# Softmax features stored head by head, with kv and numerator blocks of 4 or 5 heads instead of 8, and two kv accumulation banks instead of three

## Chip, cores, metric

One core of one Trainium2 chip. The metric is the device time of one execution in microseconds (us), from several executions of each kernel. TensorE is called PE, VectorE DVE, ScalarE ACT, GpSimd POOL. Changed and unchanged kernel are always timed in alternating rounds on the same chip.

## What is computed

Two layers, each a linear-attention block A and a gated bilinear MLP B, on x of 2048 x 576 (32 heads of 18, MLP width 4608). Cut to what matters:

```python
def _A_ref(x, wqkv, w_phi, wo):                      # H = 32, Dh = 18
    q, k, v = ...                                    # x @ wqkv, per head
    pq = einsum("bhsd,hdf->bhsf", q, w_phi);  pk = same of k
    phi_q = concat([softmax(pq), softmax(-pq)], -1)  # two branches of 18: 36 features a head
    phi_k = concat([softmax(pk), softmax(-pk)], -1)
    kv = einsum("bhsf,bhsd->bhfd", phi_k, v);  z = sum over s of phi_k
    num = einsum("bhqf,bhfd->bhqd", phi_q, kv)
    den = einsum("bhqf,bhf->bhq", phi_q, z) + 1e-6
    return (num / den) @ wo                          # heads put together
x = x + A(ln(x));  x = x + B(ln(x));  x = x + A(ln(x));  x = x + B(ln(x))
```

A 128-token tile of phi has 32 x 36 = 1152 features, which TensorE takes as 9 blocks of 128. v carries a column of ones per head, so 19 columns a head give kv and z, and numerator and denominator, together.

## The kernel before

The program is written as threads that yield operations with an assumed duration. A list scheduler fixes the order of each engine's instructions when the kernel is built, so other durations or buffers mean another order. Eight PSUM banks are a pool (`pb`). The features are ordered branch 0 of all heads, then branch 1:

```python
self.dd = A("dd", [128, self.NSM, 2, D], BF16)            # phi: branch, then head, then 18
# kv of one 128-token tile: 9 blocks in 3 banks, each block against 8 heads (152 columns)
def kv_ops(self, sm, vxs, bi, bank, first, last):
    for i in range(3):
        k = 3 * bi + i
        g0 = 7 * k                                        # a block touches heads g0 .. g0+7 (mod 32)
        parts = ...                                       # split where the heads wrap: 10 matmuls a tile
        for j, h, n in parts:
            ops.append(... e.matmul(s.ps[:, bank, c0:c0 + CW * n], phi[:, 128 * k:128 * k + 128],
                                    s.vx[:, vxs, h:h + n, :], ...))
# after all tiles: keep of each block only the head that each feature row belongs to
    em = lambda e: e.tensor_tensor(BD[:, k0:k0 + 3], kv, mask9, ALU.mult)      # 3 times, DVE
# numerators of one tile: 12 matmuls of 152, 114, 76 or 38 columns
    e.matmul(s.ps[:, bank, c0:c0 + CW * n], s.eT[:, et, k, :], s.BD[:, k, j:j + n, :], ...)
# layer 1 accumulates kv over its 16 tiles in three PSUM banks held all the while
    gots = yield ("acqn", ["pb"], 3); s.kvb = [g_[1] for g_ in gots]
```

Layer 2 adds kv pair by pair of tiles into SBUF, inside layer 1's MLP. The MLP runs in 8 blocks of 256 tokens per layer: gate and up projections as pairs of half-height matmuls, then the down projection, whose weights stream in slices (`wdr`, `wdx`). Other work is slipped between.

## Time and profile before

| | before |
|---|---|
| median of 3 runs | 1109.35 us (1108.31 to 1110.13) |
| profiled span | 1108.5 us |
| PE / DVE / ACT / POOL busy | 97 / 52 / 33 / 27% of the span |
| MLP of layer 1 begins | 119.2 us |
| one full MLP block, layer 1 / layer 2 | 62.6 / 57.1 us |

The lines this rests on, and how to read them, stand in the prediction below. The blocks are bounded by the starts of MLP matmuls in the chain that ended last (layer 1: 239.5 to 302.1; layer 2: 709.5 to 766.6).

### The profile page before, as it was taken

What the parts mean: (1) busy time and instruction counts of PE and PEld (TensorE: products, weight loads), DVE (VectorE), ACT (ScalarE), POOL (GpSimd) and SP (SyncE); (2) the same over time, 40 slices, a digit from 0 to 9 for tenths busy, and PEclk for the clock granted to TensorE, in tenths of its full rate; (3) what the DMA queues carried; (4) which work ended last, traced back from release to release, by engine and by line L of the source; (5) the groups of instructions that cost most, each with busy time, mean ns of one, the idle gap of its engine ahead of it and who ended that gap; (6) DMA issues with size and microseconds to landing.
All of it is one profiled execution on the core that took longest, in us unless ns stands there. A gap on an engine that the chain in (4) does not pass through costs nothing.

```text
span 1108.5 us, 33749 instructions
## 1 busy us (share of the span) xinstructions
PE 1074.4 (97%) x15294; PEld 827.0 (75%) x15356; DVE 579.8 (52%) x1180; ACT 369.4 (33%) x870; POOL 297.5 (27%) x318
## 2 busy tenths in 40 slices
PE   6997999999999999999999989999999999999998
PEld 4676877868687787868587678686868686868685
DVE  6989645646374664636353676444445353524231
ACT  6776522414042332404232562131313030402120
POOL 4665404314161433302320252211212030300000
PEclk9999999999999999999999999999999999999999
DMA  8475326273733627170623313817271726352504
GB/s 171 120 236 237 57 63 175 29 205 47 187 66 115 125 46 189 32 211 21 161 67 97 97 24 47 216 35 216 36 216 35 194 58 189 62 177 53 177 29 140
DMA packets 185001, 129.06 MB, mean 116 GB/s; under 512 B 103322, under 2 KB 183706, under 8 KB 183706
## 3 DMA queue, kind: packets, MB, share of 16 engines
q1 hardware_dynamic: 184858, 126.91, 45.5%
q8 instruction: 120, 1.97, 0.7%
q14 instruction: 23, 0.19, 0.1%
HBM read 100.75 MB, written 2.36 MB: 93 GB/s over the span
## 4 chain that ended last, share of the span: by engine, by line
PE 85%; DVE 8%; DMA 2%; ACT 2%; POOL 1%; issue 1%; SPq 0%; POOLq 0%; DVEq 0%
PE ps L1481 49%; PE ps L1554 20%; PE ps L1011 6%; PE ps L1556 4%; PE ps L999 3%; PE ps L1342 2%; DVE st L943 1%; DMA wdr<-in_B_w_down_dram 1%; DVE ss L1166 1%; PE ps L1219 1%; DVE mxx L1086 1%; POOL dd L1177 1%; DVE mxmn L1044 1%; DVE hT L1529 1%; DVE mxmn L1039 1%
## 5 line engine op out<-in xcount | busy, mean ns | idle before, releaser
L1481 PE MATMUL ps<-xT,Wg 64*128 64x256 bf16 x4608 | 581.3, 269 | 0.8 <-ACT xT L981 0.8
L1481 PE MATMUL ps<-xT,Wu 64*128 64x256 bf16 x4608 | 580.0, 269 | 1.1 <-DVE hT L1529 0.8
L1481 PEld LDWEIGHTS ps<-xT,Wu 64*128 64x128 bf16 x4608 | 430.8, 94 | 31.0 <-DVE hT L1529 4.2
L1481 PEld LDWEIGHTS ps<-xT,Wg 64*128 64x128 bf16 x4608 | 428.0, 94 | 32.6 <-issue 3.3
L1527 ACT CAST hT<-ps 128x512 bf16<-128x512 f32 x288 | 168.3, 584 | 564.9 <-PE ps L1481 560.5
L1529 DVE TENSOR_TENSOR hT<-ps,hT 128x512 bf16<-128x512 f32 x288 | 196.8, 689 | 213.1 <-ACT hT L1527 210.8
L1554 PE MATMUL ps<-wdr,hT 128*128 128x512 bf16 x912 | 237.0, 380 | 2.0 <-DMA wdr<-in_B_w_down_dram 2.0
L1556 PE MATMUL ps<-wdr,hT 128*128 128x64 bf16 x960 | 185.0, 193 | 3.4 <-ACT hT L1527 0.7
L1554 PEld LDWEIGHTS ps<-wdr,hT 128*128 128x128 bf16 x960 | 93.9, 98 | 112.9 <-DMA wdr<-in_B_w_down_dram 4.2
L1481 PE MATMUL ps<-xT,Wr 64*128 64x256 bf16 x1152 | 174.5, 269 | 0.0
L1177 POOL TENSOR_TENSOR dd<-dd,ss 128x576 bf16<-128x576 bf16 x119 | 136.5, 1169 | 123.5 <-ACT ss L1173 118.6
L1147 POOL TENSOR_TENSOR dd<-xT,mxq 128x576 bf16<-128x576 bf16 x56 | 63.5, 1164 | 317.8 <-DVE mxq L1143 317.8
L1597 DVE TENSOR_TENSOR x_sb<-ps,x_sb 128x64 bf16<-128x64 f32 x32 | 7.0, 219 | 229.7 <-PE ps L1556 229.7
L971 POOL TENSOR_SCALAR xln<-x_sb,nmean,rstd 128x576 bf16<-128x576 bf16 (+1 forms) x99 | 60.7, 618 | 204.5 <-DVE nmean L956 107.2
L1166 DVE TENSOR_REDUCE ss<-dd 128x64 f32<-128x1152 bf16 x61 | 82.2, 1348 | 26.6 <-ACT dd L1160 23.7
L1556 PEld LDWEIGHTS ps<-wdr,hT 128*128 128x128 bf16 x960 | 94.0, 98 | 0.9 <-DVE hT L1529 0.7
L1481 PEld LDWEIGHTS ps<-xT,Wr 64*128 64x128 bf16 x1152 | 71.9, 94 | 6.6
L1554 PE MATMUL ps<-wdx,hT 128*128 128x512 bf16 x178 | 51.6, 380 | 0.9 <-DMA wdx<-in_B_w_down_dram 0.9
L943 DVE BATCH_NORM_STATS2 st<-x_sb 128x6 f32<-128x288 bf16 x120 | 46.0, 445 | 2.8 <-DMA x_sb<-in_A_x_dram 2.7
L1158 ACT ACTIVATE dd<-dd 128x576 bf16<-128x576 bf16 x49 | 33.5, 684 | 37.9 <-DVE dd L1058 27.5
L999 PE MATMUL ps<-Wq,xT 128*128 128x288 bf16 x300 | 40.1, 286 | 1.4 <-DVE dd L1058 1.4
L1011 PE MATMUL ps<-Wo,oT 64*128 64x288 bf16 x504 | 40.0, 283 | 0.0
(135 smaller groups left out, 960.4 us busy)
## 6 DMA issues: line engine op xcount, KB each, us to landing
wdr<-in_B_w_down_dram SPq DMA_DIRECT2D x240, 288.0 KB, 3.6
wdx<-in_B_w_down_dram SPq DMA_DIRECT2D x48, 288.0 KB, 3.7
Wg<-in_B_w_gate_dram SPq DMA_DIRECT2D x4, 1152.0 KB, 13.1
Wu<-in_B_w_up_dram SPq DMA_DIRECT2D x4, 1152.0 KB, 15.7
x_sb<-in_A_x_dram SPq DMA_DIRECT2D x8, 288.0 KB, 3.2
out_dram<-x_sb SPq DMA_DIRECT2D x16, 144.0 KB, 2.4
Wraw<-in_A_wqkv_dram SPq DMA_DIRECT2D x8, 144.0 KB, 3.0
xT<-xln SPq DMA_TRANSPOSE x58, 2.7
```

The source lines that it names most:

```text
L943: ops.append(Op(d_dve(288), (lambda e, j=j, h=h, src=src: e.bn_stats(st[:, sl[j], 6 * h:6 * h + 6], src)), reads=rd, writes=[("st", sl[j], ...
L971: em = [(lambda e, j=j, a=a, b=b, c=c: e.tensor_scalar(xln[:, sl[j], a:b], x_sb[:, ss[j], c:c + b - a], s.nmean[:, sl[j]:sl[j] + 1], rstd[ ...
L999: full = [Op(d_pe(N), (lambda e, k=k, h=h: e.matmul(s.ps[:, banks[h], 0:N], L[:, k, :], Wm[:, k, N * h:N * h + N], start=(k == 0 and fresh ...
L1011: out.append(Op(61, (lambda e, h=h, k=k, st=(i == 0 and k == 0), sp=(i == 1 and k == 3): e.matmul(s.ps[:, banks[h], 0:N], L[r, k, :], Wm[r ...
L1147: yield ("ops", "pool", [Op(1150, (lambda e, d=d, mb=mb: e.tensor_tensor(d, p3, mb, ALU.subtract)), reads=[("xT", st_), ("mq", mq, br)], w ...
L1166: Op(1265, (lambda e: e.tensor_reduce(ss[:, sm, :].rearrange("p (b g) -> p b g", b=2), e4, AX.X, ALU.add)), reads=s.ddk(sm, 0) + s.ddk(sm, ...
L1177: yield ("alt", [(eng, [Op(dur, (lambda e, ev=ev, rb=rb: e.tensor_tensor(ev, ev, rb, ALU.mult)), reads=s.ddk(sm, br) + [("ss", sm)], write ...
L1481: out.append(Op(54.3, (lambda e, bank=bank, cs=cs, lhsT=lhsT, rhs=rhs, st=st, sp=sp: e.matmul(ps[:, bank, cs].rearrange("p (a n) -> p a n" ...
L1527: yield ("ops", "act", [Op(480, (lambda e, gb=gb, p=p: e.copy(hT[:, p, :], ps[:, gb, :])), reads=[("gu", gb)], writes=[("hT", p)] + (s.raw ...
L1529: yield ("ops", "dve", [Op(600, (lambda e, ub=ub, p=p: e.tensor_tensor(hT[:, p, :], ps[:, ub, :], hT[:, p, :], ALU.mult)), reads=[("gu", u ...
L1554: ops = [Op(d_pe(512), (lambda e: e.matmul(s.ps[:, bank, 0:512], lhsT, s.wslot(slot)[:, fi, 0:512], start=(f == 0), stop=(f == NF - 1))), ...
L1556: Op(d_pe(64) + 3, (lambda e: e.matmul(s.ps[:, z, 64 * sl:64 * sl + 64], lhsT, s.wslot(slot)[:, fi, 512:576], start=(f == 0 and (sl == 0 o ...
```

## The change

The intent is fewer columns for PE. With both branches of a head side by side, a block of 128 features covers 4 or 5 heads instead of 8, so more than 40% of the columns, all of which the mask had set to zero, need not be computed. The core of the diff:

```diff
-        self.BD = A("BD", [128, NK, GH, CW], BF16)
-        self.kvacc = A("kvacc", [128, NK, KW], F32)
+        self.BD = A("BD", [128, 2, KC], BF16)              # KC = 5*4*19 = 4*5*19 = 380
+        self.kvacc = A("kvacc", [128, 2, KC], F32)
-        self.dd = A("dd", [128, self.NSM, 2, D], BF16)
+        self.dd = A("dd", [128, self.NSM, H, 2, DH], BF16)
+def kblock(k):
+    i = k // 2
+    return (7 * i, 4, 4 * CW * i) if k % 2 == 0 else (7 * i + 3, 5, 5 * CW * i)
 ...
-        de1 = dd[:, sm, 0, :]                              # likewise in every use of dd
+        de1 = dd[:, sm, :, 0, :]
 ...
-        for i in range(3):
-            k = 3 * bi + i
-            ...
+        for k in range(bi, NK, 2):
+            h, n, c0 = kblock(k)
+            ops.append(... e.matmul(s.ps[:, bank, c0:c0 + CW * n], phi[:, 128 * k:128 * k + 128],
+                                    s.vx[:, vxs, h:h + n, :], ...))
 ...
-        gots = yield ("acqn", ["pb"], 3)
+        gots = yield ("acqn", ["pb"], 2)
```

The masks follow (one memset and four mask operations more on POOL at the start, 1.6 us together), and kv, masking and accumulation run over 2 banks instead of 3.

## The prediction

> **What bounds the kernel now.** I read the page first: engine shares, the 40 slices and the shares of the chain that ended last.
>
> ```profile
> span 1108.5 us, 33749 instructions
> PE 1074.4 (97%) x15294; PEld 827.0 (75%) x15356; DVE 579.8 (52%) x1180; ACT 369.4 (33%) x870; POOL 297.5 (27%) x318
> ...
> PE   6997999999999999999999989999999999999998
> ...
> DVE  6989645646374664636353676444445353524231
> ...
> PEclk9999999999999999999999999999999999999999
> ...
> PE 85%; DVE 8%; DMA 2%; ACT 2%; POOL 1%; issue 1%; SPq 0%; POOLq 0%; DVEq 0%
> ```
>
> TensorE (PE) is the bound of nearly everything, at full granted clock. The exception is the first four slices (27.7 us each), where VectorE is as full as PE. A busy PE proves little, because matmul records overlap, so I took busy times over chosen stretches (the columns are stretch and length, then PE, weight load, DVE, ACT and POOL busy with instruction counts, clock, DMA share, GB/s):
>
> ```profile
> 75.00:90.00 15.00, 10.76 (x107) 8.04 (x106) 13.63 (x22) 8.85 (x25) 7.61 (x7) 1.00 1.02 427
> ...
> 176.00:612.00 436.00, 431.70 (x6510) 337.12 (x6536) 235.85 (x476) 138.43 (x316) 131.86 (x140) 1.00 0.45 108
> ...
> 709.00:1108.00 399.00, 392.54 (x5859) 300.62 (x5883) 161.19 (x314) 92.33 (x178) 60.00 (x64) 1.00 0.45 116
> ```
>
> There are two regimes. Until about 98 us the k softmax of layer 1 runs: DVE has 13.6 of 15 us, and PE waits. From 119 us on, PE streams the gated MLP with attention work slipped in between; in 176 to 612 only 4.3 of 436 us have no matmul in flight, while DVE, ACT and POOL have at least 46% of that stretch to spare. A nanosecond of matmul taken out of this regime should come off the end; one taken out before 98 us mostly should not.
>
> The third view is the groups by shape, for the two lines the change shrinks: L1219 (kv = phi_k^T times v) and L1342 (numerator = phi_q times the masked kv).
>
> ```profile
> L1342 PE MATMUL ps<-BD,eT 128*128 128x152 bf16 x192 | 25.3, 229 | 1.0 <-ACT eT L1318 1.0
> L1219 PE MATMUL ps<-vx,dd 128*128 128x152 bf16 x200 | 20.3, 230 | 3.1 <-POOL dd L1177 2.4 <-DVE dd L1177 0.8
> L1342 PE MATMUL ps<-BD,eT 128*128 128x114 bf16 x64 | 13.5, 211 | 0.0
> L1342 PE MATMUL ps<-BD,eT 128*128 128x38 bf16 x64 | 11.7, 183 | 0.0
> L1342 PE MATMUL ps<-BD,eT 128*128 128x76 bf16 x64 | 7.4, 198 | 0.0
> ```
>
> The means (183 to 230 ns) are latencies and must not be multiplied by counts. What a matmul takes from PE is the step from one start to the next, read from the timeline (start, length, group):
>
> ```profile
> 634.14 1.17 PE L1219 MATMUL ps<-vx,dd 128*128 128x152 bf16 x17 [0.40 <-POOL dd L1177]
> 635.15 2.61 PE L999 MATMUL ps<-Wq,xT 128*128 128x288 bf16 x20
> 637.60 0.78 PE L1342 MATMUL ps<-BD,eT 128*128 128x152 bf16 x12
> 638.22 1.39 PE L999 MATMUL ps<-Wq,xT 128*128 128x288 bf16 x10
> ```
>
> Seventeen kv matmuls (13 of 152 columns, 4 of 76) give way after 1.01 us, and the twelve numerator matmuls of one tile after 0.62 us.
>
> **What the Trainium skill says.** "TensorE: Matmul & The Clock Gate", section "Wait — 56ns, not 53.3ns?": back-to-back warm matmuls step by N/2.4 GHz plus about 2.5 ns, with a floor of about 25 ns. The trace agrees: 13 x 65.8 + 4 x 34.2 = 992 ns against 1.01 us, and 6 x 65.8 + 2 x 50 + 2 x 34.2 + 2 x 28 = 619 ns against 0.62 us; I use 28 ns as the floor, because the down projection's pair of 512 and 64 columns repeats about every 0.24 us (220.38, 220.62 in the timeline), which leaves about 28 ns for the 64. The same page, "Back-to-back issue gap", warns that pairs of weight load and matmul sustain only about 81 ns at 128 columns. If that held, short matmuls would gain nothing. The trace disagrees: nine 128-column transposes, each with its own weight load, start at 98.49 and give way at 99.00, 57 ns each. So weight loads should not hide the gain. "GPSIMD Engine Reference", "Performance pitfalls for Q7 kernels", puts a cost on reads whose inner step exceeds 8 bytes. The new layout strides the outer dimension only; the inner step stays one bf16, so POOL should not change.
>
> **The change part by part.**
> A 128-feature block used to touch 8 heads (branch 0 of all heads, then branch 1); with a head's two branches adjacent it touches 128/36 = 3.6 heads, in practice 4 or 5.
>
> kv, per tile of 128 tokens. Before: 9 blocks x 152 = 1368 columns in 10 matmuls, 8 x 65.8 + 2 x 34.2 = 595 ns. After: 5 x 76 + 4 x 95 = 760 columns in 9 matmuls, 5 x 34.2 + 4 x 42.1 = 339 ns. Saved: 256 ns.
>
> Numerator, per tile. Before: 619 ns, above. After: one block of 4 straddles head 16 and splits into 2 x 38, so 10 matmuls: 4 x 34.2 + 4 x 42.1 + 2 x 28 = 361 ns. Saved: 258 ns.
>
> Where they lie. There are 16 tiles in each of two layers. Layer 2's kv, and the numerators of both layers, run after 98 us, beside the PE-bound MLP or in the short chains around 101 to 119 and 634 to 651 us, where they stand on the chain too: 16 x (256 + 258 + 258) = 12.4 us. Layer 1's kv (16 x 256 = 4.1 us) runs before 98 us under DVE; the chain passes through it only now and then (0.6 to 0.8 us pieces), so I count a quarter, 1.0 us.
>
> Masking kv into BD at the end of layer 1 is 3 DVE operations of 626 ns on 456 elements, on the chain at 96 to 98 us. After: 2 on 380 elements, about 546 ns each (626 less 76 elements at 1.04 ns, an estimate from the DVE rows of 288 and 512 elements, 455 and 689 ns: 234 ns for 224 elements). Saved: 0.8 us. Layer 2's accumulation on DVE falls from 24 x 605 ns to 16 of about 526, 6.1 us of DVE, hidden behind PE: 0.
>
> Moves without expected cost: DVE, ACT and POOL now touch phi in runs of 18 with a stride of 36. The trace has such forms already: ACT writes v into runs of 18 at stride 19 in 401 ns, the same as a contiguous copy of 288 (401); DVE reads the numerator that way in 455 ns against 452. Four more mask-building POOL operations fall in the start-up: at most 1 us of POOL, probably hidden.
>
> Sum: 12.4 + 1.0 + 0.8 = 14.2 us off 1109.35, 1.3%.
>
> **Rivals.**
> (a) The gain gets lost in waits. If PE finishes earlier but each block's layer norm, weight slices or PSUM evacuation do not, PE idles instead. Against: PE waits in the steady part are tenths of a microsecond per block, and DMA moves about 110 GB/s with slices at 230 elsewhere. For: w_down waits stand on the chain (about 5 us of transfer at 357, 604 and 868), and the chain passes through the layer norm's statistics in each layer 2 block. A quarter lost gives 1098.5; all lost gives 1109.
> (b) The reordering matters more. Instruction order is fixed at build time from assumed durations, and tuning values chosen for the old order stay. New durations and a freed PSUM bank (two held through layer 1 instead of three) reshuffle the start-up, where between 17 and 105 us some 9 us pass with no matmul in flight (88 less the 79.0 us of PE busy in six stretches). With more banks k and q projections can run ahead: I allow 5 us better, and as much worse for a bad interleaving. "Perfetto Trace Analysis", "Optimization Strategy", says consistent bubbles can mean too little PSUM; here the bubbles sit behind DVE, so I expect little from the bank itself.
> (c) Strided phi makes POOL's multiplies (1169 ns, 119 of them) or ACT's exponentials slower. At 10% it adds about 0.25 us of POOL per tile; only layer 1's 16 tiles would show it, up to 4 us: 1099.
>
> **Range and chances.** From 14.2 I take off 2 us for (a) and the other frictions and leave (b) centred on zero: 12.2 us, 1097. The best case with all of layer 1's kv and a better start-up is 1087 to 1088; a bad reshuffle with losses is about 1107. A gain over 2% needs the time below 1087.2, beyond all the matmul time removed (16.5 us) plus 6 more: 6%. Slower by 2% needs 34 us of new waits: 1%.
>
> **What would show it.** The kv and numerator groups should appear with 76, 95 and 38 columns; a tile's numerators should give way after about 0.36 us, and its kv after 0.34. A layer 1 block (62.6 us from 239.5 to 302.1) should shrink by about 1.0 us, a layer 2 block (57.1 us from 709.5 to 766.6) by 0.5. The MLP should begin (119.25 us now) 1 to 3 us earlier, and the rows of POOL, ACT and DVE on phi keep their means. I am wrong if short matmuls step by well over 45 ns (weight loads bind), if blocks keep their length with new PE waits, or if the MLP begins at a time off by more than 5 us.

## The result

| | before | changed |
|---|---|---|
| median | 1109.28 us (4 runs) | 1095.01 us (4 runs, 1094.49 to 1096.43) |
| profiled span | 1108.5 us | 1092.9 us |
| MLP of layer 1 begins | 119.2 us | 115.5 us |
| first MLP block | 57.5 us | 58.8 us |
| full MLP block, layer 1 / layer 2 | 62.6 / 57.1 us | 61.6 / 56.6 us |

The ratio is 0.9877, 95% interval 0.9863 to 0.9891: 1.2% faster. A ratio here is the mean time of one kernel's fast runs over the mean of the other's in the same rounds, so not quite the ratio of the medians. Two repetitions of the changed kernel gave 0.9870 and 0.9875; the mean of the three is 0.9874, or 14.0 us of 1108.5. All runs of this study were in the fast state.

The page of the changed kernel (span, busy shares, chain by engine):

```profile
span 1092.9 us, 33612 instructions
PE 1061.4 (97%) x15260; PEld 811.7 (74%) x15260; DVE 571.2 (52%) x1171; ACT 367.7 (34%) x864; POOL 304.0 (28%) x327
...
PE 84%; DVE 9%; DMA 3%; ACT 2%; issue 1%; SPq 0%; POOL 0%
```

PE is the bound as before. The groups by shape for the numerators (L1351 is the old L1342):

```profile
L1351 PE MATMUL ps<-BD,eT 128*128 128x76 bf16 x128 | 17.1, 199 | 0.9 <-ACT eT L1327 0.9
L1351 PE MATMUL ps<-BD,eT 128*128 128x95 bf16 x128 | 14.8, 206 | 0.3 <-DVE BD L1296 0.3
...
L1351 PE MATMUL ps<-BD,eT 128*128 128x38 bf16 x64 | 6.6, 181 | 0.0
```

The three shapes are the predicted ones. The latencies fell by only 10%; the steps between starts tell the gain. Timeline of PE for one tile's numerators in the MLP, then, from the chain in order of time (start, length), one tile's kv:

```profile
219.27 0.52 PE L1351 MATMUL ps<-BD,eT 128*128 128x76 bf16 x10
219.63 0.38 PE L1563 MATMUL ps<-wdr,hT 128*128 128x512 bf16 x1
```

```profile
73.11 0.34 PE ps L1229 x9
```

The numerators give way after 0.36 us (predicted 0.361), and the kv after 0.34 us (predicted 0.339). Weight loads do not bind here: nine matmuls of 76 or 95 columns, each with its own load of 128 columns, step every 38 ns on average.

Busy times over MLP blocks, before: first block, a full block of layer 1, one of layer 2.

```profile
119.10:176.70 57.60, 57.39 (x864) 44.07 (x868) 27.32 (x57) 15.10 (x32) 12.95 (x14) 1.00 0.45 106
239.50:302.10 62.60, 62.34 (x942) 48.90 (x946) 35.48 (x74) 20.05 (x46) 20.80 (x22) 1.00 0.46 112
709.50:766.60 57.10, 56.72 (x849) 43.51 (x853) 25.62 (x52) 14.17 (x28) 11.52 (x12) 1.00 0.49 122
```

The same of the changed kernel:

```profile
115.40:174.40 59.00, 58.76 (x860) 44.33 (x862) 28.34 (x60) 14.26 (x30) 13.96 (x14) 0.97 0.41 104
359.50:421.10 61.60, 61.55 (x941) 47.88 (x940) 34.78 (x73) 20.06 (x46) 20.96 (x22) 1.00 0.46 114
753.50:810.10 56.60, 56.43 (x849) 43.00 (x848) 25.62 (x52) 14.17 (x28) 11.60 (x12) 1.00 0.48 122
```

A layer 1 block is 1.0 us shorter (two tiles of kv and two of numerators, 2 x 514 ns), a layer 2 block 0.5 us (two of numerators, 2 x 258 ns). The first four full blocks of layer 1 took 62.6 to 63.1 us before and 61.6 to 62.0 after. The first block did not shrink: it is 1.3 us longer, and its mean granted clock (third number from the right) is 0.97. That was not foreseen. The timeline of PE just before that block shows why. Before the change, two tiles' q projections (20 matmuls) stood between the two sets of six transposes:

```profile
113.78 0.56 PE L979 MATMUL ps<-ident,xln 128*128 128x128 bf16 x6
114.28 2.62 PE L999 MATMUL ps<-Wq,xT 128*128 128x288 bf16 x20
116.74 0.56 PE L979 MATMUL ps<-ident,xln 128*128 128x128 bf16 x6
```

After the change nothing does, because the projections were ordered earlier, and PE waits 2.01 us for a layer norm:

```profile
111.51 0.56 PE L993 MATMUL ps<-ident,xln 128*128 128x128 bf16 x6
114.09 0.57 PE L993 MATMUL ps<-ident,xln 128*128 128x128 bf16 x6 [2.01 <-DVE xln L985]
114.73 0.54 PE L1351 MATMUL ps<-BD,eT 128*128 128x76 bf16 x10
115.48 0.28 PE L1490 MATMUL ps<-xT,Wg 64*128 64x256 bf16 x1 [0.21 <-ACT xT L995]
```

Stretches of the same execution, where the clock is again the third number from the right:

```profile
111.60:115.45 3.85, 1.59 (x23) 0.97 (x21) 1.59 (x7) 2.94 (x9) 0.00 (x0) 1.00 0.30 44
115.45:117.00 1.55, 1.52 (x18) 1.15 (x20) 1.41 (x5) 0.13 (x1) 1.34 (x2) 0.60 0.00 0
117.00:119.00 2.00, 2.00 (x22) 1.47 (x20) 2.00 (x3) 0.00 (x0) 1.23 (x2) 0.50 0.00 0
```

PE had a matmul in flight for 1.59 of 3.85 us, most of that transposes, and for 3.4 us after that the clock was granted at one half, at the very moment the MLP began. The Trainium skill describes this ("TensorE: Matmul & The Clock Gate", "What's actually happening": idle drops the clock to half, judged over free-running windows of about 3.4 us); the trace agrees with the length of 3.4 us.

### The profile page after: what moved, and what is told of

The parts are those of the page before. It is cut to its first block, busy times and chain, and to the rows that moved or that the text cites. A ratio compares the mean times of both kernels' runs of the same rounds, so it can differ in the third digit from the quotient of the medians.

```text
span 1092.9 us, 33612 instructions
## 1 busy us (share of the span) xinstructions
PE 1061.4 (97%) x15260; PEld 811.7 (74%) x15260; DVE 571.2 (52%) x1171; ACT 367.7 (34%) x864; POOL 304.0 (28%) x327
## 4 chain that ended last, share of the span: by engine, by line
PE 84%; DVE 9%; DMA 3%; ACT 2%; issue 1%; SPq 0%; POOL 0%
PE ps L1490 49%; PE ps L1563 21%; PE ps L1025 6%; PE ps L1013 3%; PE ps L1565 3%; DVE ss L1180 2%; DVE st L957 2%; DMA wdr<-in_B_w_down_dram 1%; DVE mxx L1100 1%; PE ps L1351 1%; DMA wdx<-in_B_w_down_dram 1%; DVE hT L1538 1%; DMA x_sb<-in_A_x_dram 1%; PE ps L1229 1%; DVE mxmn L1058 1%; DVE mxmn L1053 1%
## 5 line engine op out<-in xcount | busy, mean ns | idle before, releaser
L1563 PE MATMUL ps<-wdr,hT 128*128 128x512 bf16 x960 | 244.7, 380 | 0.9 <-DMA wdr<-in_B_w_down_dram 0.9
L1191 POOL TENSOR_TENSOR dd<-dd,ss 128x576 bf16<-128x576 bf16 x119 | 139.1, 1190 | 124.0 <-ACT ss L1187 121.1
L1161 POOL TENSOR_TENSOR dd<-xT,mxq 128x576 bf16<-128x576 bf16 x56 | 63.6, 1166 | 306.8 <-DVE mxq L1157 306.8
L985 POOL TENSOR_SCALAR xln<-x_sb,nmean,rstd 128x576 bf16<-128x576 bf16 (+1 forms) x103 | 63.0, 616 | 196.4 <-ACT rstd L974 97.7
L1563 PE MATMUL ps<-wdx,hT 128*128 128x512 bf16 x192 | 54.3, 380 | 0.5 <-DMA wdx<-in_B_w_down_dram 0.5
L1187 ACT ACTIVATE ss<-ss 128x64 f32<-128x64 f32 x116 | 29.8, 257 | 31.5 <-DVE ss L1180 30.4
```

What stands on the lines that cost most here:

```text
L985: em = [(lambda e, j=j, a=a, b=b, c=c: e.tensor_scalar(xln[:, sl[j], a:b], x_sb[:, ss[j], c:c + b - a], s.nmean[:, sl[j]:sl[j] + 1], rstd[ ...
L1161: yield ("ops", "pool", [Op(1150, (lambda e, d=d, mb=mb: e.tensor_tensor(d, p3, mb, ALU.subtract)), reads=[("xT", st_), ("mq", mq, br)], w ...
L1191: yield ("alt", [(eng, [Op(dur, (lambda e, ev=ev, rb=rb: e.tensor_tensor(ev, ev, rb, ALU.mult)), reads=s.ddk(sm, br) + [("ss", sm)], write ...
L1563: ops = [Op(d_pe(512), (lambda e: e.matmul(s.ps[:, bank, 0:512], lhsT, s.wslot(slot)[:, fi, 0:512], start=(f == 0), stop=(f == NF - 1))), ...
```

## The experiments

Theory: PE's column time made the gain, in full after the start-up and in part within it. Rivals: the freed bank and the new order made it; part of the columns hides behind waits; the half clock gave some of it back. In the "columns back" runs the added matmuls are unknown to the scheduler (assumed duration 0). I compared the instruction lists: every engine has exactly the changed kernel's order, with only the added matmuls between (320 more among 15374 PE instructions with all columns back, nothing else different). They write unused PSUM columns, so results stay right. Differences in us below are differences of ratios times 1108.5. Each ratio has an interval of about 0.0015 (1.6 us) on either side unless given, so a difference of two is less certain still. The three sets of rounds ran on different chips; the first had no changed kernel in it, so its runs are set against the mean of the three.

### All columns given back

```diff
+        if extra:                                   # kv: columns 380.. of the bank, never read
+            for k, h0, n in ((bi, 0, 6), (bi + 2, 6, 6), (bi + 4, 12, 4)):
+                ops.append(Op(0, ... e.matmul(s.ps[:, bank, KC:KC + CW * n], phi[:, 128*k:128*k+128],
+                                              s.vx[:, vxs, h0:h0 + n, :], start=False, ...)))
+        for i, k in enumerate((0, 1, 6, 7)):        # numerators: columns 304.. of the two banks
+            ops.append(Op(0, ... e.matmul(s.ps[:, banks[i // 2], 16*CW:24*CW], s.eT[:, et, k, :],
+                                          s.BD[:, k % 2, 0:8*CW], start=False, ...)))
```

> The changed kernel, every instruction in the same order on every engine, with matmuls into unused PSUM columns that give back the columns the change took away: per tile 6 more for kv (4 of 114 columns, 2 of 76; about 268 ns) and 4 more of 152 for the numerators (about 263 ns). Theory (the gain is PE column time after the start-up): layer 2's kv gives 16 x 0.268 = 4.3 us, the numerators 32 x 0.263 = 8.4 us, layer 1's kv about a quarter of 4.3: 13.8 us in all, so about 1109 us, ratio to the kernel before 0.998 to 1.002. Rival (freed PSUM bank and new instruction order made most of it): less than half of the 14 us comes back, under 1102 us.

Measured: 1109.09 us median (13 runs), ratio 0.9999 (0.9989 to 1.0008). 13.9 us came back, the whole gain. New layout, new order, second bank and fewer DVE operations, taken together with the long columns, are worth nothing within about 1.2 us (1.7 us if one allows that the added matmuls cost 0.5 us more than those removed: 32 x (268 + 263) against 32 x (256 + 258) ns). The theory holds as a whole.

### The parts one by one

The same edit in one place only: kv of layer 2, numerators of both layers, kv of layer 1 (twice). The changed kernel itself ran beside them as a baseline.

> The changed kernel itself once more, on the same chip and in the same rounds as the three others, as their baseline. Expected ratio to the kernel before 0.9877, as measured already, within 0.0014.

> The changed kernel, order unchanged, with 6 more matmuls per tile that give back the columns of kv in layer 2 only (16 tiles x 268 ns). Theory (PE-bound stretch, everything counts): 4.3 us slower than the changed kernel, ratio 0.9916. Rival (part of PE's time is slack around the waits for w_down slices): under 3 us.

> The changed kernel, order unchanged, with 4 more matmuls of 152 columns per tile that give back the columns of the numerators in both layers (32 tiles x 263 ns). Theory: 8.4 us slower than the changed kernel, ratio 0.9953. Together with layer 2's kv (4.3) and layer 1's (1.2 measured) the parts should add up to the 13.5 to 14 us that came back with all columns. Rival (the parts hide behind one another): sum under 11 us.

> As the run with all columns given back, but only in layer 1's kv (16 tiles x 268 ns = 4.3 us of PE before the MLP starts), order unchanged. Theory (that stretch waits on VectorE, a quarter is on the path): about 1.1 us slower than the changed kernel, 1096. Rival (the start-up is as PE-bound as the rest): 4 us or more, 1099. Second rival (wholly hidden): 1095.

> The changed kernel a third time, as the baseline of the three other runs of this call: ratio to the kernel before between 0.986 and 0.989. Of its executions profiled so far one had the half clock at the start of the MLP and one had not, after the same pause of PE; which it is here is open.

> The same kernel as kv1_back, repeated beside the changed kernel in the same rounds because 1.1 and 2.2 us could not be told apart. A quarter of 4.3 us on the path: 1.1 us slower than the changed kernel; half of it, as the MLP start of the first run's trace suggests: 2.1 us; all: 4.3 us.

| run | median us (runs) | ratio to before | changed kernel's ratio | slower by | matmul time added |
|---|---|---|---|---|---|
| changed kernel, again | 1093.78 (4) | 0.9870 | | | |
| kv of layer 2 back | 1098.07 (5) | 0.9909 | 0.9870, same rounds | 4.3 us | 4.3 us |
| numerators back | 1103.27 (6) | 0.9955 | 0.9870, same rounds | 9.4 us | 8.4 us |
| kv of layer 1 back | 1096.90 (4) | 0.9888 | 0.9874, mean of three | 1.6 us | 4.3 us |
| changed kernel, third time | 1094.66 (4) | 0.9875 | | | |
| kv of layer 1 back, repeated | 1096.93 (4) | 0.9898 | 0.9875, same rounds | 2.5 us | 4.3 us |

After the start-up the added time came back in full, as far as the runs can tell: 4.3 of 4.3 and 9.4 of 8.4 us. Set directly against the changed kernel's runs of the same rounds, these are uncertain by about 0.8 and 1.9 us (95%). Before the MLP about half counted: 2.0 us of 4.3 as the mean of two runs. That agrees with the traces, where the MLP begins at 117.7 us in both executions with layer 1's columns back, against 115.5, 116.4 and 115.5 in three of the changed kernel. It is likely more than the quarter I had assumed, but the times alone don't exclude a quarter: the repetition, set directly against its changed kernel, gives 2.4 us with 1.5 on either side, so between 0.9 and 3.9. The parts add up to 15.7 us where all at once gave 13.9; the intervals are too wide to say whether that is real. Some of these traces (all columns back, numerators back, the second of layer 1) also show 7 to 10 us of half clock between 12 and 23 us. The two executions with layer 1's columns back, one with it and one without, begin the MLP at the same 117.7 us, so at that place it cost nothing that can be seen.

### A third bank held

```diff
-        gots = yield ("acqn", ["pb"], 2)
+        gots = yield ("acqn", ["pb"], 3)            # the third is never used
```

> The changed kernel, but layer 1 holds a third PSUM bank that nothing uses, as before the change (so the build-time order of the start-up differs). Theory (the bank matters little): 1095 within 1.5 us, MLP start within 1.5 us of 115.5. Rival (the MLP started 3.7 us earlier because a sixth free bank let projections run ahead): MLP start back at 117.5 to 119, but no pause of PE of 2 us before it and no fall of the clock, so the time may rise by only 0 to 2 us.

> The same kernel as third_bank, repeated beside the changed kernel in the same rounds. In its trace two tiles' q projections moved from the start-up into the first MLP block, which then began its successor 2.8 us later than in an execution of the changed kernel without the half clock. If that is the bank's worth the time is about 2 to 3 us above the changed kernel; if the bank is worth little, under 1 us.

Measured: 1097.00 and 1097.53 us (4 runs each), ratios 0.9888 and 0.9903, that is 1.6 us slower than the mean of the changed kernel and 3.1 us slower than it in the same rounds. The first alone was inconclusive. In the second no run is as fast as any of the changed kernel, so this kernel is slower; the mean of the two is about 2.4 us. Holding the bank, with the order that follows from it, costs something after all. The MLP begins at 116.8 us, 0.4 to 1.3 us later, and with less done: the groups of its first block in the second run show 36 half-height q-projection matmuls, which that block of the changed kernel does not have.

```profile
L1025 PE MATMUL ps<-Wo,oT 64*128 64x288 bf16 x36 | 2.9, 283 | 0.0
L1025 PE MATMUL ps<-Wq,xT 64*128 64x288 bf16 x36 | 2.9, 282 | 0.0
```

They are the projections of two tiles, about 2.5 us of PE. With a sixth free bank they are done before the MLP begins. Neither run has the half clock at the MLP's start, but both have it elsewhere in the start-up: for 3.4 us at about 88 us in both, for 3.4 us at about 67 us in the second and for 6.8 us from 14 us in the first. The three traces of the changed kernel have none at these places. So part of the 2.4 us can be the clock, and what the bank alone is worth stays open. The kernel also differs in order from the changed kernel, so bank and order can't be parted here. It is not additive either: with all columns back two banks gained nothing. Why is open; that the longer matmuls fill the very pauses that the projections would use is only argued.

### The pause filled

```diff
+        fill = [Op(0, ... e.matmul(s.ps[:, bank, 0:512], s.ident[:], s.Wv[:, 0, 0:512], ...))
+                for _ in range(8 if sig[0] == ("xTB2", 1) else 0)]
-        yield ("ops", "pe", [ ...six transposes of the second tile... ])
+        yield ("ops", "pe", fill + [ ...six transposes of the second tile... ])
```

> The changed kernel with 8 matmuls of 512 columns (8 x 216 ns = 1.7 us), whose result nothing reads, put into PE's 2.0 us pause just before the second tile's transposes at 112 us; order otherwise unchanged. Theory (the pause lets the granted clock fall to half for 3.4 us once the MLP has begun, which costs half of that): the first block of the MLP shrinks from 58.8 to about 57.0 us, the clock there is 1.00, and the time falls by about 1.7 us to 1093.3. Rival (the clock falls anyway, or the fall is an accident of this one execution): the time stays at 1095 within 0.7 us.

The timeline of PE in the profiled run (one of the eight matmuls is missing from the trace):

```profile
112.03 0.56 PE L996 MATMUL ps<-ident,xln 128*128 128x128 bf16 x6
112.75 1.67 PE L994 MATMUL ps<-Wv,ident 128*128 128x512 bf16 x7 [0.16 <-ACT x_sb L1418]
114.60 0.57 PE L996 MATMUL ps<-ident,xln 128*128 128x128 bf16 x6 [0.18 <-DVE xln L986]
```

The first block took 57.2 us with a clock of 1.00, as expected. The time, 1094.42 us (4 runs), ratio 0.9865, is 1.0 us below the mean of the changed kernel, which the intervals don't resolve. The repetitions of the changed kernel tell one reason why it is less than the block's 1.6: in one of three profiled executions the clock did not fall, after the same wait of 2.01 us. Its stretch after the MLP's start:

```profile
115.50:119.00 3.50, 3.15 (x60) 2.75 (x60) 2.96 (x8) 0.85 (x2) 2.44 (x3) 1.00 0.00 0
```

There the first block took 57.2 us. Over all eight profiled executions of kernels with this order (three of the changed kernel, five with columns back) the clock fell seven times; in the three with the pause filled and the two with a third bank it never fell at this place. So with the new order the half clock falls on the MLP's start in most executions but not all, and costs about 1.6 us there. That size comes from the blocks, 58.8 against 57.2 us. The times point the same way: of the 12 executions of the changed kernel, the four with a mean clock of 0.999 or more took 1093.9 us on average, the other eight 1094.9.

That the old order is free of it is not shown. Its one trace has full clock throughout, but of the 35 later executions of the kernel before, 30 had a mean clock below 0.999, which leaves room for 3.4 us or more at half clock somewhere. Where, no trace shows.

### A better version

By the sizes of its tiles the change freed 1792 bytes of SBUF per partition, which with a little shuffling makes room for a sixth slot of down-projection weights (a slot takes 2304 bytes, so part of the room was free before). In the MLP of the changed kernel PE waits for such slices (times and counts):

```profile
PE ps L1563 <- DMA wdr<-in_B_w_down_dram: 0.9, 3, 0.6
...
PE ps L1563 <- DMA wdx<-in_B_w_down_dram: 0.5, 2, 0.3
```

```diff
-        ... self.NWD, self.NO, self.NOT = 2, 4, 2, 2, 2, 5, 1, 2
+        ... self.NWD, self.NO, self.NOT = 2, 4, 2, 2, 2, 6, 1, 2
-        self.den = A("den", [128, self.NO, H], F32)
+        self.den = AT("den", [128, self.NO, H], F32, nc.lookup_mloc(self.wtpad).addr)
         # and the filled pause of the run above
```

> An attempt at a better version: the filled pause, and a sixth full-time slot for w_down slices in the SBUF that the change freed (the reciprocal's small tile moves into the padding). Expected: the filling gives about 1.3 us as measured, the extra slot takes away PE's waits for w_down slices (three or four of 0.3 to 0.7 us, 1.4 us in all in the changed kernel): 1092.5, ratio 0.985. Rival (the slices come late because their transfers are issued late, or the order shifts): no gain over the filled pause, 1094.

> The same kernel as warm_wd6, repeated: 2.1 us below the changed kernel of the same rounds (as the medians of the first time), no wait of PE for a w_down slice after the start-up, no half clock at the start of the MLP. Rival (the first time was luck): within 0.7 us of the changed kernel.

Measured: 1091.72 (1090.51 to 1092.69) and 1091.13 us (1090.59 to 1091.93), ratios 0.9849 and 0.9846. The changed kernel of the same rounds had 1093.78 and 1094.66 us; the ranges of single runs don't overlap. It is 2.3 and 3.2 us faster by the ratios, and the fastest version of this study. After the start-up PE's list of waits holds one wait of 0.3 us for a slice in the first run and none in the second. How much of the gain is the slot and how much the filled pause was not parted, and the instruction order differs too.

## Why the prediction was right

It said 1097 us, with 1087 to 1088 as the best case and about 1107 as the worst, and gave 7% to a change of more than 2% either way. The time was 1095.0, and 1093.8 and 1094.7 in the repetitions.

- **Steps between starts, not latencies.** Right to the digit: 0.36 and 0.34 us a tile. The warning of 81 ns for pairs of weight load and matmul did not apply.
- **12.4 us of PE time after the start-up count in full.** Right within the noise: giving back layer 2's kv and the numerators cost 4.3 and 9.4 us for 4.3 and 8.4 us of matmuls; the blocks shrank by the predicted 1.0 and 0.5 us.
- **"I count a quarter, 1.0 us"** of layer 1's kv. Probably too small: about half, 2.0 us as measured on the slightly longer matmuls given back, though the times don't exclude a quarter. The stretch is DVE-bound on average, but kv stands on its chain often enough.
- **Masking, 0.8 us.** The operations went from 3 x 626 to 2 x 536 ns (predicted 546). What that alone is worth was not tried.
- **Layout for free.** Nearly: ACT's exponentials kept 413 ns and went from 684 to 688; POOL's multiplies went from 1169 to 1190 ns (1.8%, not rival (c)'s 10%), 119 of them, 2.5 us of an engine that is 28% busy. With the columns back the new layout ran as fast as the old kernel. The masks took five more POOL operations and 1.6 us, not four and at most 1 us.
- **"I expect little from the bank itself."** Doubtful: the kernel that holds a third bank is about 2.4 us slower, but its order and its clock in the start-up differ too. The allowance of 5 us for the start-up covered it. The predicted MLP start, 1 to 3 us earlier, was 2.8 to 3.7 us earlier, beyond that range in two of three traces.
- **"I take off 2 us for (a) and the other frictions."** This step failed: the measured gain of 14.0 us is the 14.2 before the deduction, not the 12.2 after it. The waits on weight slices, (a)'s main case, did not grow: PE waited 2.9 us for slices after 119 us in the trace before, and 1.3 to 1.8 us in the three traces of the changed kernel. A loss of that size that I had not named does occur, the half clock of about 1.6 us in most executions. What layer 1's kv gave beyond a quarter, and perhaps the bank, made up for it, so the closeness of the sum is partly luck. (A slip that changes nothing: a quarter of 14.2 us lost gives 1098.7, not 1098.5.)

## What to carry to other kernels

To price short matmuls, take the step from one start to the next, and ask which stretch they stand in; in the PE-bound stretch the whole of it came off the end, before it about half. Columns that a mask sets to zero can often be avoided by reordering features, at little cost for elementwise engines as long as the inner runs stay contiguous. When work is taken out of a latency-bound stretch just ahead of the dense matmuls, look at the pauses that open there: a stretch of 3.85 us with PE busy for 1.59 was enough, in seven of eight profiled executions, to start the dense part at half clock.

## What the Trainium skill lacked or had wrong

- "TensorE: Matmul & The Clock Gate", "Back-to-back issue gap", gives about 81 ns per matmul of 128 columns for sustained pairs of weight load and matmul. Here nine such pairs took 57 ns each, and nine of 76 or 95 columns 38 ns each (0.34 us), each with its own load of 128 columns. These are bursts of nine; a longer stream was not measured.
- The same page, "Why this matters for your kernels", asks to avoid PE pauses above about 3 us between bursts. Here a longest wait of 2.01 us, with PE busy 1.59 of 3.85 us, led to 3.4 us of half clock in seven of eight profiled executions; in the eighth the same wait did not. The page may still hold: without the transposes, the gap between PE's other matmuls was 2.9 to 3.1 us, with the half clock at both ends of that range. Whether transposes count as activity was not tested.
- No page read here gives a POOL elementwise operation whose operands are strided in the outer dimension: the multiplies on runs of 18 at a stride of 36 took 1190 ns for 576 elements, against 1169 contiguous, while the subtractions that write such runs kept theirs (1164 to 1166).
- No page read here says what a spare PSUM bank is worth to a statically ordered kernel: here a kernel that held one more was about 2.4 us of 1094 slower, with two tiles' projections later, but bank, order and clock were not parted.
